# A new order and a new choice of engines for a two-layer attention and mixer kernel

## The chip, the cores and the metric

The kernel runs on one core of one Trainium2 chip. The metric is the device time of one execution in microseconds (us): 437.09 us for the kernel before, the median of three runs (436.16 to 437.51). One execution was also profiled; every time below that is not called a run's time comes from that one.

The engines are written as in the profile: PE multiplies matrices (PEld loads its weights), ACT, DVE and POOL work on elements, SP issues the DMA transfers. The engines run side by side. Each takes its own instructions strictly in order, and an instruction may wait on semaphores that other engines or transfers raise.

## What is computed

Two layers, each a sliding-window attention block and a token-mixing MLP, over one sequence of 2048 tokens with 512 features (cut to what matters):

```python
def _A_ref(x, wqkv, wo):                      # H = 32 heads of 16, window 256
    qkv = ((x @ wqkv).reshape(B, S, 3, H, Dh)).transpose(2, 0, 3, 1, 4)
    q, k, v = qkv[0], qkv[1], qkv[2]
    scores = jnp.einsum("bhqd,bhkd->bhqk", q, k) * (Dh ** -0.5)
    mask = (idx[:, None] - idx[None, :] >= 0) & (idx[:, None] - idx[None, :] < W)
    p = softmax(where(mask, scores, -1e9))
    return (einsum("bhqk,bhkd->bhqd", p, v)).transpose(0, 2, 1, 3).reshape(B, S, D) @ wo

def _B_ref(x, w1, b1, w2, b2):                # mixes along the tokens; F = 1792
    u = gelu(einsum("bsd,sf->bdf", layernorm(x), w1) + b1)
    return (einsum("bdf,fs->bds", u, w2) + b2).transpose(0, 2, 1)

x = A_x
for _ in range(2):
    x = x + _A_ref(layernorm(x), A_wqkv, A_wo)
    x = x + _B_ref(layernorm(x), B_w1, B_b1, B_w2, B_b2)
```

## The kernel before, in words

The program first records a graph of 2476 operations (`Graph.op`). An operation is one or a few instructions on one engine, with what it reads and writes; some operations have alternatives (`alts`) on other engines. The string `ORDER` then says in which sequence all operations are put down and, for each, which alternative is taken. `Graph.replay` follows it: it appends each operation to its engine's list and gives out the buffers (eight PSUM banks, pools of SBUF tiles) in that sequence. `Graph.emit` writes the lists out with the waits that the data and the reuse of buffers need. So `ORDER` alone decides the order on every engine, the engine of the operations of free choice, and which earlier user a buffer waits for. No cost is read at this point: the costs in the code were of use to the search that made the string, which is not part of the kernel.

The operations that the text speaks of, in the order in which a block of tokens meets them:

- x and the projection weights are loaded at the start (`load_x` L401, `load_w` L405; the weights of Q, K and V come in pieces: K first half, Q first half, V, K second half, Q second half, a half being 256 columns, that is two of four groups of eight heads).
- Layer norm: statistics L471 and L473 on DVE, the inverse root L484 on POOL, the normalised block L491 on DVE.
- The normalised block is transposed: for the first 512 tokens of layer 0 on PE (L549) with a copy out of PSUM on DVE (L556) or ACT (L558), later by a DMA (`tr`, L542).
- Projections on PE (L513). Q goes out of PSUM by DVE (L572) or ACT (L574). K goes straight into the buffer `kbd` (two instructions, DVE L583 or ACT L582), or into a staging tile `stg` (DVE L594, ACT L596) and from there into `kbd` by POOL or DVE (L609, two instructions) or by eight DMAs of SP (L604). V goes out by DVE (L631) or ACT (L633) and then by four DMAs into `vb` (`vz`, L636).
- Attention goes in 152 score operations on PE (L690). Each fills two pairs of PSUM banks; two exponentials on ACT (L705) empty them into a tile of `pt`. Masks (L726) multiply parts of `pt` on POOL or, with an AND, on DVE. When all parts of a group of heads are there, PE multiplies by V (`pv`, L747). DVE transposes the result (L767), takes a reciprocal (L771), POOL or DVE forms the product (L773), DVE transposes back (L778). PE applies `wo` (L513) and DVE adds to x (L789).
- The mixer: partial sums over the tokens that are ready (`u_part`, L513, out by DVE L853/L857 or ACT L855) are filled in between; the last part (L868) follows after attention, then an addition (L879, DVE), gelu (L883, ACT), and the second product (L513) with its addition to x (L909, DVE). The weights come in by SP (L803, L815). In layer 1 the results go out block by block (L955, L898).

PE never waits for PE. The score operations keep ACT busy, and everything else on PE is put between them, so that ACT has scores to work on and PE has something to do while ACT works.

Of the kernel before, what the change touches and what calls it, by code (L numbers as in the profile page):

```python
# [11 lines left out]
P = 128  # L12


ORDER = (
    'c-qBQJ&5a87Cw^iym#m24ro9DE$D$>P@zHr1r$&~4;*kn0Tl{p!G#}q!G!|~IH1A-2lN&PwBQ9TIN-tyE*x;-!V50EV3sLdcwrV?xbVUhQ@EI7Sf+5{!o?nq'
    '$20ciz5Hx8yJyB%_g-CH-SeIAd`ALMAW$=FmRTW@UM>_MC=^Pi;EO_mPE}Ps8;@00Q*G-bFh2xcf8YPD^Jy4{4r?wJVNeNZF(i;5j)u<AALc&kTb8BtuoYXD'
    'EV9&YSZ!4!>!g`bN{ewkFV?-!CZqniE{d#Ft%9xV!b#)(TCEaPYV5=_a)q2Md&JD;Y}-<ZEX(4%qNtz|nGh-nqM(nNFd2`>41lrbFj=oV>y08w5=@sO5l;Q9'
    'E5~t`4k7c4g`?**4MwApcs`k)PYEH@>2%p2_m%ug%J;zU^<}w}Bmj_HTwbUu%%gUDrPRKHF)ZpZ8V-j>IkgT#q9zGxwOWL+*Q6H5QAD5FVugcBIS8UCVtAx5'
    'oJ<&u19$iv7cna1#_*YKJ5^OyJ|z~OtkC_q)3F@aao}aY-|XcJja+V-4ePd#=6Nr5$8=54^GwtKgfnf&d1+c%n=zA#x^CzI129br?M|l+Elo!hRD}YZf_Qqu'  # L20
    'SP)3ERD?p|W-T+p<AlWmmz&J>+$%~ixu#_`=S`xiFBAY-2B_6)1cnJql2x_3URO7ptD9B5K6*wd)Vkd{-aVgQFQ<Q>cFUdVVsW`#OsA3K%;)o&*{hi55Q9-J'
    '&$FfBG&||^{?_aDDLp%bAP7veKNy<kcP63}C9PHz{n0aH$ElgsxDhjE)LBq-b-g0Gt{ca(`sEk$b^TQ&DrE65;-xkz7100?E&w~1%|a*V<m_xVrnDCQ9!bX-'
    'm1YXX*h}M)fU!Om&@okIOl(PvC5<{j12J|S3bq}Tigu~!`;_{gMNNZdeg7q;j;bwzsGwS!B?u~0Ziq%Y!^?{V8oI8Zce{fD0`^>Em^H0dLzbj46plFn<Ww=A'
    'FQK`4LOj>DNP1RH&t|jQXq06s1sG+39kbi*t^uyE!Cc~!i-kgzrhK_Xo{tGG>%nMzHqPfML1rY`Bx!fr#C02P^EJAFZ(cjutY58xXXjs)hPF-A3lBL3pX4lJ'
    'o4RQ@9~cBgQ$#}$1OcwgE@B2$AdHBjArra3DN3SFkg5WD1k-axgz>l%2E(u)1b&%$CBINMT;FsZMb~r1oPiq~IYiJfbj!AeLw#WAgbe9`w0dBuuGqvgRI6$j'
    'Lc4<2z`#YeO+!o3Fn0_>IzT9qQcL7U7do+6@7L?yx^*Vrn%pXe80Su@MFqwhm|>=H;=0V37#a(!ArlQI2rlNJAe`WqOfhG#%;{=H-5W~sx^x5=7q*a+gflh$'
    'eZw$Pt#TZr6a%Qw`y4VQmouyne9JOS0EC7qvVzDPj44PKNl{G8B<pp1eIlAyme0J)%S%H$)eL|an)+N(`aLv4B*F~_HO#v|s2W6@$RDsi$nbjkB_tw<aCUYk'
    '2%!wcfUen!F_|78BN06ngymAB$TM;-Nt5|()|t)vvzaWn&qvv;Tm`7MhvtWaKA@`N30<K-=(ly9A_Jd|R8$)In<f)_y+1(=bS0n$TwlMwx<cq7j=u@(C`omM'
    's+WpyhcVx0`At5b6!LM*{CvrmDw0$xmkNc#rysW*%d#2dEs#FcKqmsA;wpwx&^1K`SfV3>fB;P<6ID1nqf~>FlQsVIBw?qUO$1{_QR7&{n2;j^pNrDz@KvRP'
    'TuK<mIr4oZ1y_!9SyUwYJ76btI<*!T3yU5b?QZw{9Hy=d9K2`0HxPs}^t#>t;Lp8&uVtQFrU}$Q`lqt{ZNl~Yf`ICa&~-Y75XsujO{=A87$B%rB7GV}b(9zY'  # L30
    '!{`(WoNg6MMP0AzkT0PA69N(@pXYm16Wzfq^z*(fYqEw}a{7X?cLkw<Ig%y~Rv3X&ok}t$2N6%!f^;N~$NkaC$qf0x1Uyf>-6bt(Dr%$g90?}?KF5_9Bjq&r'
    '9VRfOm7H#+>+RW`V$C>FkB<j`i7}q|K(_<XYPW`Ah;7)b*Etl+sQ&d=xDeCKb@TZ=swXnG*RcqAC>3m#2FEZ|10}nJyGwXDa!fJMLOcUE@4D;t8rCTF_KdDp'
    '|1^yA<<&pVaphmfWICUu<!>~UB*XY_G#-s?$tqjlN}AScVXSKL*K!D9S_VJ=yjH4~LRu`AgEE#cl(BpvpVe)WwLK4sNQCSM`bXp=iwJ^1G+BAkm!89|;E<#0'
    '5m!-^W`k?os-6+90>f~bsiaDi{tQqkm1!RJ6VNdN6KJ;<Xrpm^*cw#FsDIU@*6DORRU@vZyI^4JQ7JM?MU+}7R=i5t^UGK(hjfISwCi<9P;1@T^KGmPwx6?$'
    '*`}Si72oo#we1*=ty>Z<K|oE*NRs|kQo3VFj-qBWDr2RP%}Py=YhYMbK*X6DDpU<N!bV@P(lwST5xh&(i+Q7GS|c{pKw4GeK!HfSMw)Ln+D&j%-rOMigkF)W'
    'tIbAOU&8!+J`XM&6!y_r8jXS!q*_hOK?T1v(t@EBna)rd<f<%4h$aS4NQ;jOl%l*~OW_w9_o&0&&v3hj+gnZ!duhI<*Czn)Jlx^9hb0`)bV%+FN`XV$Zku+n'
    '%>ZN|?LN&sO}kq=zHOhv-X((zp6<=U-J8*Pa_H5QU5DrIHq7vcHy#^*d!K)d4tMK5e>l${9Ua~EIN<K_y7Py7!t>njX^wjX)W6uc-L~877SOvn4xM=XCjR#3'
    'ffxM4i0An?kYc;%9Wwk|$-{APJ07>ksr#_L-FWzK8n-+D0aDygj{&!b@9tr^=Pk!^+<%y7KZ6b2k1gcj|6*(}X#Cwjf54*cklzn(I)3MF&FvFM_fPP5OiFd)'
    'PDWB$dFT6#-?q>0yM*KRNS1zT!}g1NyGbT<D<hdyr!twhb1?I;1+K~*&h7>o9{)0XkL(?vf4BgDKjPoOZ+@F@{L_OaPq}pBkzPEK;jMa+EjG7q-XVq8Cxq-~'
    'fqY-CA5M)9kj(yDwjO2Pn4mw1SmuWW<UnaM{7ypdNwS?t+e|9Z`@ub6^$)5i|0od;xd4x4`DbU#p|J1k!A{$`U5U8saSyKSuRIv-&+SBsdzd5tlMLqG#I842'  # L40
    'njg9Q>mP6%x*dvl<9p-|jZg3K-1a{$!)bv|s~^WdEIxed;iHG!)%)G|$*<zszX32A5e)'
)

def begin_order(n):
# [944 lines left out]
```

## Time and profile before

| what | value |
|---|---|
| median of three runs | 437.09 us (436.16 to 437.51) |
| the profiled execution, its time as a run | 436.27 us |
| its span in the profile | 434.5 us |
| granted PE clock | 1.00 in every stretch |
| busy: DVE, ACT, POOL | 322.6 us, 317.0 us, 187.2 us |
| DMA | 46.03 MB, mean 106 GB/s |

In the page of the profile the span is cut into 40 slices of 10.9 us; each digit is an engine's busy share in tenths. The span is shorter than the run's time by 1.8 us, which lies around the program and is not part of it. "Busy" of PE counts a matmul from its start to its modelled end, so that pauses shorter than a matmul's pipeline do not show as idle.

### The profile page before, as it was taken

To read this page: it belongs to the slowest core of one execution; us is meant where nothing else is said; L and a number is where in the kernel's file an instruction comes from. 1 tells how busy PE (TensorE), PEld (TensorE's weight loads), DVE (VectorE), ACT (ScalarE), POOL (GpSimd) and SP (SyncE) were. 2 spreads that over 40 slices of the span, in tenths; PEclk is the share of its full clock that TensorE was granted. 3 is DMA by queue.
4 is the path that set the end of the run, shared out by engine and by line. 5 is a ranking of instruction groups with operands and counts; after the bars stand their busy time and mean duration, and the time that the engine had idled before them with its cause. 6 is when DMAs were issued, how large, how long until landed. Compare 5 with 4: busy or idle time off the path is not lost.

```text
span 434.5 us, 14318 instructions
## 1 busy us (share of the span) xinstructions
PE 420.9 (97%) x6177; PEld 188.5 (43%) x6177; DVE 322.6 (74%) x629; ACT 317.0 (73%) x364; POOL 187.2 (43%) x277
## 2 busy tenths in 40 slices
PE   7979989999999999999999999999999999999997
PEld 6534333434444444444444444444434444445443
DVE  7998989779996678556777999989788758422205
ACT  5999999999997953606999999899999870520000
POOL 7788865864664620011465554365435221000000
PEclk9999999999999999999999999999999999999999
DMA  8565262302163257723542282240223262747713
GB/s 237 167 125 88 63 127 37 79 5 49 26 166 83 75 152 211 208 62 88 137 110 52 64 147 64 51 77 11 47 64 99 66 175 69 226 140 213 228 32 115
DMA packets 101850, 46.03 MB, mean 106 GB/s; under 512 B 32156, under 2 KB 101788, under 8 KB 101788
## 3 DMA queue, kind: packets, MB, share of 16 engines
q1 hardware_dynamic: 101788, 45.13, 41.7%
q8 instruction: 49, 0.80, 0.8%
q14 instruction: 13, 0.11, 0.1%
HBM read 33.56 MB, written 2.10 MB: 82 GB/s over the span
## 4 chain that ended last, share of the span: by engine, by line
PE 73%; ACT 18%; DVE 6%; DMA 1%; POOL 1%; issue 0%; SPq 0%
PE PS L513 50%; ACT pt L705 17%; PE PS L868 8%; PE PS L690 8%; PE PS L747 7%; DVE stats L471 1%; DMA vb<-vst 1%; DVE xh_sb L491 1%; DVE pt L726 1%; DVE rl L767 1%; DMA x_sb<-in_A_x_dram 1%; POOL pt L726 0%; DVE stg L594 0%; DVE vst L631 0%; SPq L636 0%
## 5 line engine op out<-in xcount | busy, mean ns | idle before, releaser
L705 ACT ACTIVATE pt<-PS 128x1024 bf16<-128x1024 f32 (+1 forms) x304 | 281.0, 1036 | 13.1 <-PE PS L690 11.9
L726 POOL TENSOR_TENSOR pt<-pt,ldm 128x256 int32<-128x256 int32 (+2 forms) x189 | 125.9, 686 | 101.7 <-ACT pt L705 101.1
L513 PE MATMUL PS<-xhT,wqkv 128*128 128x512 bf16 (+1 forms) x288 | 67.8, 357 | 2.7 <-ACT pt L705 1.9
L513 PE MATMUL PS<-xh_sb,w1b 128*128 128x512 bf16 x280 | 69.9, 381 | 0.1
L513 PE MATMUL PS<-uT,w2b 128*128 128x512 bf16 (+2 forms) x308 | 68.3, 360 | 0.0
L690 PE MATMUL PS<-qT,kbd 32*128 32x64 bf16 (+4 forms) x1552 | 60.2, 247 | 3.1 <-ACT pt L705 2.1
L484 POOL TENSOR_TENSOR rstd<-agg,mhalf 128x2 f32<-128x2 f32 (+1 forms) x33 | 23.8, 722 | 66.8 <-DVE agg L473 66.7
L909 DVE SCALAR_TENSOR_TENSOR x_sb<-PS,bcol,x_sb 128x512 bf16<-128x512 f32 x31 | 22.6, 746 | 38.0 <-PE PS L513 37.7
L690 PEld LDWEIGHTS PS<-qT,kbd 32*128 32x128 bf16 x1552 | 22.7, 92 | 61.7 <-ACT pt L705 45.6
L767 DVE STREAM_TRANSPOSE rl<-PS 128x1024 f32<-128x1024 f32 x32 | 39.9, 1248 | 12.3 <-PE PS L747 12.1
L747 PE MATMUL PS<-pt,vb 64*17 64x128 bf16 (+4 forms) x3104 | 43.6, 248 | 2.4 <-DMA vb<-vst 1.1
L471 DVE BATCH_NORM_STATS2 stats<-x_sb 128x6 f32<-128x512 bf16 x64 | 44.2, 693 | 1.5 <-DMA x_sb<-in_A_x_dram 0.8
L883 ACT ACTIVATE uT<-rl,bcol 128x512 bf16<-128x512 f32 x28 | 18.3, 712 | 33.8 <-DVE rl L879 33.8
L513 PEld LDWEIGHTS PS<-uT,w2b 128*128 128x128 bf16 x308 | 27.5, 98 | 31.1 <-issue 3.2
L747 PEld LDWEIGHTS PS<-pt,vb 64*17 64x17 bf16 x3104 | 31.8, 84 | 17.6 <-issue 7.9
L513 PE MATMUL PS<-uT,pt 128*128 128x512 bf16 x168 | 39.2, 379 | 0.0
L868 PE MATMUL PS<-xh_sb,w1b 128*128 128x512 bf16 x168 | 37.7, 379 | 0.0
L513 PEld LDWEIGHTS PS<-xhT,wqkv 128*128 128x128 bf16 x288 | 24.2, 97 | 30.1 <-issue 6.3
L513 PEld LDWEIGHTS PS<-xh_sb,w1b 128*128 128x128 bf16 x280 | 23.7, 98 | 30.8 <-issue 5.9
L513 PE MATMUL PS<-wqkv,xhT 128*128 128x512 bf16 x128 | 34.2, 381 | 0.2 <-DVE stg L594 0.2
L726 DVE TENSOR_TENSOR pt<-pt,ldn 128x256 int32<-128x256 int32 (+1 forms) x77 | 29.6, 404 | 5.3 <-ACT pt L705 5.0
L513 PE MATMUL PS<-wo_sb,oT 128*128 128x512 bf16 x128 | 32.4, 380 | 0.5 <-ACT pt L705 0.5
(62 smaller groups left out, 340.7 us busy)
## 6 DMA issues: line engine op xcount, KB each, us to landing
w1b<-in_B_w_dram SPq DMA_DIRECT2D x112, 128.0 KB, 2.8
w2b<-in_B_w_dram SPq DMA_DIRECT2D x70, 128.0 KB, 2.8
pt<-in_B_w_dram SPq DMA_DIRECT2D x42, 128.0 KB, 3.0
vb<-vst SPq DMA_DIRECT2D x64, 68.0 KB, 2.1
out_dram<-x_sb SPq DMA_DIRECT2D x15, 128.0 KB, 1.8
x_sb<-in_A_x_dram SPq DMA_DIRECT2D x3, 512.0 KB, 6.2
kbd<-stg SPq DMA_DIRECT2D x80, 16.0 KB, 1.9
wqkv<-in_A_wqkv_dram SPq DMA_DIRECT2D x4, 256.0 KB, 5.4
```

Of the source, the lines that this page charges most:

```text
L471: op("vector:stat", lambda e: e.bn_stats(st[:, 0:6], x_sb[:, t, :]), reads=[f"x{t}"], writes=[("st", i)], cost=dve_cost(512))
L484: op("gpsimd:rstd", lambda e: e.tensor_tensor(rstd[:, t0:t1, 0], agg[:, t0:t1, 1], mhalf[:, 0:1].to_broadcast([P, t1 - t0]), op=ALU.pow), ...
L491: op("vector:xh", lambda e: e.tensor_scalar(xh_sb[:, t, :], x_sb[:, t, :], agg[:, t, 0:1], rstd[:, t, :], op0=ALU.subtract, op1=ALU.mult), ...
L513: return e.matmul(o, lhsT=w, rhs=x, start=start, stop=stop, skip_group_check=True)
L690: last = e.matmul(bank(tt[r // 2], r % 2)[:, base + c0 * 64:base + (c0 + n) * 64], lhsT=kbd[32 * r:32 * r + 32, tk.slot, o, jj].rearrange( ...
L705: op("scalar:exp", lambda e, ts=ts, tp=tp, i=i, cols=cols: e.activation(probs(tp)[:, i, 0:cols, :], pair(ts)[:, :, 0:cols].rearrange("p r ...
L726: return e.tensor_tensor(v, v, m, op=by)
L747: last = e.matmul(bank(t, h)[32 * r:32 * r + 17, i + q0 * 64:i + (q0 + n) * 64], lhsT=vb[64 * h:64 * h + 64, tk.slot, jj, 4 * o + r, :], r ...
L767: op("vector:od", lambda e, t=tod, tr=tr: e.transpose(rl[:, tr.slot:tr.slot + 2].rearrange("p a b -> p (a b)"), pair(t)), reads=[(tod, i) ...
L868: last = e.matmul(bank(tu, tt), lhsT=v()[:, sc - b0, k0 + tt * P:k0 + (tt + 1) * P], rhs=xh_sb[:, sc, :], start=(sc == b0), stop=(sc == NT ...
L883: op("scalar:gelu", lambda e, ft=ft, tt=tt: e.activation(uT[:, ft, :], rl[:, tmps[tt].slot], ACTF.Gelu_apprx_tanh, bias=b1col[:, ft:ft + 1 ...
L909: op("vector:resy", lambda e: e.scalar_tensor_tensor(x_sb[:, t, :], bank(ft), b2col[:, t:t + 1], x_sb[:, t, :], op0=ALU.add, op1=ALU.add), ...
```

## The change

Only the string `ORDER` differs: the sequence of the 2476 operations and the alternative of each were found anew, in a search in which all larger transfers and all operations of free choice were assumed to take longer than measured.

```diff
 ORDER = (
-    'c-qBQJ&5a87Cw^iym#m24ro9DE$D$>P@zHr1r$&~4;*kn0Tl{p!G#}q!G!|~IH1A-2lN&PwBQ9TIN-tyE*x;-!V50EV3sLdcwrV?xbVUhQ@EI7Sf+5{!o?nq'
...
+    'c-p;IL5S<t6}`{%{O8Tj8_)*@6wn8KP(T4Kl%jxAR8T-4Tu?v@1)SoA0}g26fC3IU;DRX*IK=^f&_Wa!TyVfGF3iG|S$N@v3r=xi0$$8w3NCozfD5yjg$uLj'
...
 )
```

Decoded, the choices of engine that change (operations, not instructions):

| operation | before | after |
|---|---|---|
| K out of PSUM into `stg` | ACT 3, DVE 24 | ACT 4, DVE 23 |
| K out of PSUM into `kbd` | ACT 4, DVE 5 | ACT 2, DVE 7 |
| Q out of PSUM | ACT 7, DVE 29 | ACT 10, DVE 26 |
| V out of PSUM | ACT 5, DVE 27 | ACT 7, DVE 25 |
| partial sums of the mixer out of PSUM | ACT 3, DVE 39 | ACT 2, DVE 40 |
| `stg` into `kbd` | POOL 12, DVE 5, SP 10 | POOL 12, DVE 6, SP 9 |
| masks | POOL 189, DVE 77 | POOL 183, DVE 83 |
| products L773 | POOL 18, DVE 14 | POOL 23, DVE 9 |
| ones in `vst` (L458) | POOL | DVE |

PE has the same 6177 matmuls in both, and its list has the same number of changes between kinds of work: 142 from a score operation to projections or mixer, 121 the other way, 31 from `pv` to a score operation, 27 into `pv`, and so on, all equal. The sequence differs nearly everywhere in detail. The start, decoded (the operations of one engine from left to right, `sc` a score operation, K0 to K3 and Q0 to Q3 the projections of the four groups of heads, V a half of a V projection, T a transposition on PE; a token half follows in brackets where it is the second 256 tokens):

```
SP  before  x1 x0 x2-3 K01 Q01 x4-7 Q23 K23 V  b1 b2 x8-11 w1 w1 x12-15 vz tr tr tr tr wo w1 vz
SP  after   x1 x0 Q01 x2-3 K01 Q23 x4-7 K23 V  x8-11 b2 w1 w1 w2 w1 w1 b1 x12-15 w1 vz tr tr tr tr w1 w1 vz wo
PE  before  T1 T0 K0 Q0 Q1 K1 sc T3 T2 Q3 sc Q2 K2 sc K3 V b V sc V V Q3(2) sc Q2(2) sc Q0(2) K0(2) K2(2) K1(2) V sc
PE  after   T1 T0 K0 Q0 Q1 K1 sc Q3 T3 K2 T2 Q2 K3 sc Q2(2) V V sc V V sc K0(2) V V K3(2) sc K1(2) b Q0(2) sc
ACT before  L558 L558 L582 L574 L574 L596 L705x3 L574 L705x7 L574 L705x2 L582 L705 L633 L705x13
ACT after   L558 L582 L574 L574 L596 L705x2 L558 L574 L705 L596 L574 L705x5 L633 L705x2 L582 L705x17
```

More of the change, by code (lines that the diff above doesn't have):

```diff
@@ L15 @@
 ORDER = (
-    'c-qBQJ&5a87Cw^iym#m24ro9DE$D$>P@zHr1r$&~4;*kn0Tl{p!G#}q!G!|~IH1A-2lN&PwBQ9TIN-tyE*x;-!V50EV3sLdcwrV?xbVUhQ@EI7Sf+5{!o?nq'
-    '$20ciz5Hx8yJyB%_g-CH-SeIAd`ALMAW$=FmRTW@UM>_MC=^Pi;EO_mPE}Ps8;@00Q*G-bFh2xcf8YPD^Jy4{4r?wJVNeNZF(i;5j)u<AALc&kTb8BtuoYXD'
-    'EV9&YSZ!4!>!g`bN{ewkFV?-!CZqniE{d#Ft%9xV!b#)(TCEaPYV5=_a)q2Md&JD;Y}-<ZEX(4%qNtz|nGh-nqM(nNFd2`>41lrbFj=oV>y08w5=@sO5l;Q9'
-    'E5~t`4k7c4g`?**4MwApcs`k)PYEH@>2%p2_m%ug%J;zU^<}w}Bmj_HTwbUu%%gUDrPRKHF)ZpZ8V-j>IkgT#q9zGxwOWL+*Q6H5QAD5FVugcBIS8UCVtAx5'
@@ L20 @@
[L20 to L39, printed above, removed]
@@ L40 @@
-    'fqY-CA5M)9kj(yDwjO2Pn4mw1SmuWW<UnaM{7ypdNwS?t+e|9Z`@ub6^$)5i|0od;xd4x4`DbU#p|J1k!A{$`U5U8saSyKSuRIv-&+SBsdzd5tlMLqG#I842'
-    'njg9Q>mP6%x*dvl<9p-|jZg3K-1a{$!)bv|s~^WdEIxed;iHG!)%)G|$*<zszX32A5e)'
+    'c-p;IL5S<t6}`{%{O8Tj8_)*@6wn8KP(T4Kl%jxAR8T-4Tu?v@1)SoA0}g26fC3IU;DRX*IK=^f&_Wa!TyVfGF3iG|S$N@v3r=xi0$$8w3NCozfD5yjg$uLj'
+    '^~9dB=l`VnP3WDmB|Y7D-@Esmd!A!i0QPAepkf+^5#~!J8s+n09&(fd3*H-fo+R~{^A2r;^>+S)I_F$aX;g|>%X-_IOeXxo(}EzE6Ak0Uu>8O^O;?DY8gCj&'
+    '>&<fG)4CzjdP5W$9pK#JqA;D-YBk}JB#lno^3#FeeNCg(39?y*HL8(UtOkKBvruBM+Ad>`ZRrLT1WmsZR0Ra4s0tUw`OFZ8LqQlafesSd>^7U6_pTIKYAvNm'
@@ new lines @@
+    'TFj*x|A+7M<#Jgnc^(Th)9KW4I&IqTpPlt5=*-8Hadwi0pso%EgLZF8mwsBow8hC}dAY3DDwV2Mu4&-HXbhnY4LHf?&=S&Ww?t8Fz1#9?)dna4QB<i&Qn8qh'
+    'LpcmdwN?!alu}NI;b0JkAqD51Tn=oTdhdcC`2H`SIxROzM()rYv|Y!v?M4H~Eh}r8zUTS=ugoB8J~bV8`2b(qj_Wv%i3J2f(*PJqf9v%nqX%8R)zU@X&;@~W'
+    'RZ~F(I4%~8AW2d#cd0DZz~xSkOhsl28TWWTZ-Hqsl0Iw5bx8)`7>%)VIsSJUpxG=#Y5C9PY(8Ji=iPQ8tkp`nY`Y4JI9>vbE@tz;jz&q6i>K%37hj*b2)B89'
+    'Iv5UyqoGqMO!2PYKP{X}lGE?tn0aj$P6q|E*L-H0*`!uWlEgHFATX0wQZso_EPq<!Tr8E<C<s&$xuL37AqW;9lq(m(dqHqD2|o;jLRf(CPiCXh_=^_+fa3zR'
@@ new lines @@
+    'U9=`+wpsm+WpR@;NnzuO2*N-Zh>rwC(X@6OlE<9KaSV{OIAzpvTo>%fMh@o)ZiG^%8-;?aQ_ZGGTWULsdVS4Q%4A9fSyt)A<9R&qw@=zkl2qDg*Sp<%LsgXH'
+    'S0za(M(K6Wa2|%mFw3)7H0x(P@I2QC7`wV|T)M-d3$nC^hn$?805>|sxQ6A5f5UanFjgyQCxGB09Kw{35$7aMk~r>l{~Uh_6#16RBcGDQ67x>{S*?a_K#~=U'
+    'H2NfPe8<VY9|Rf77&y8uX*wW1tC1v1J*g~7qSzKi9K!Gs7JyPk@?B}zs8cYcTo#8Z%|kt3pmyG&5$Hxv)EzU>1db_%hJmRn%4(%xC#srOwNz7+WD_Js&eCAc'
+    '6sg~mdI{%k5JV)CRf5PbMo|>U#X3_3j=Ob$S~*!ZWEmSwluXO)^?Iy(TJLmv^?E&NL933`u&iOOKZs-wOkitkJp01sc;(#l^h_q>WhTB+I+i&LX`w(>m9fj!'
@@ new lines @@
+    '3UkW1?xR!Mx9xX+;k0QQBVpIr)hhMhLQ(S!md@KWZOL*mA44vi>ARXIsj6w(U>S-5x~|EBAQRLcw3_^y@yNKk0zt*zdV@{jjJyW$2t+I@9JQORRtu8)?~W0w'
+    'QmG9P!u241Dl3<la^sr@mQ;tDfEEP0d<-B+jzD3-ebgk*$MgAI6c)>cdc=q{lBVaVPCfbW^0+k^IL=UhTtdl`3K*pWUjhLnKs&Z=NK7!G5j1;3qt_J#-4X<q'
+    '(Jt+hTJ;Kd8<*$v^5>*hDpgCUNVrs)^OKVT3If8RHK7Cwi6Eqz9FoQr6^f#R@?sf5U}<YWfeK^QR#mXDfQs@4ybhByO;?dq61<99(d~AR1W{O`9{h_#tu}%R'
+    'qbN3uMXfcL<qAwes6@g?$iQJTz(V*D<2a$r5@@;&_jC6{d^8NAbE`L*9E}TKnb@79w}!*u=SW1HaRR@GB%pCZX#+R+41y*eP7j)m7+WHK_J#ZzT^kl<wOVN!'
@@ new lines @@
+    'RTs@BrF96yN@b`N3fS3L{yaYCbE+!p7}E7TB?E>5Cg_Z*uQRoeD%kxaZoDdC|3{RDn#Q@pa0|F~+ZH%A@SwRygB6~VqBIx?3{GaVnZ{HV+qkXiNdjy8EzS@T'
+    'u6+I&n2q;Gx~?B-$d#X&MCf!n=NIQV!g;f)%#{9VzfaTjOWNsn0KpAAAtn~KDwVK)c3v(gN$5CXq0o3=$rnx2E9CQ*13}iX4AcizT}l%6AAj;hl;y|adVMS}'
+    'WJ%Tug4NaX^78Vg-9&`&Z29$ad3FYLj1W06`U=H+gj+SFLBIWnzTVSuvmH^a*Q6#iy1iff9whMb$Db5GDjt=EX{o?UP|RfTCjt2RylXg4&dFvG4cjuY7iEyv'
+    '$DH{3lk+FyV^NG{XtO5L{t?O<l`bMuD#0YW!b8I0H>H9#z!kAQVQj>ay8xmfj28Hd0HBY0S&C=?KBgQNqXePM7n@Po&96bF46;EHicUVC4;Z$buZIrsQ*~^u'
@@ new lines @@
+    'Pe^;sSVyD?y;e2?Gt^AWRefL6G+E7<MMG6pnpI__1y^NRVV9Ja@w#BNN}bi>dckV!(w;4sAZt#}R;}6WY9<cA!gjb^&iHIGo0o)1eN6jsb>&~PTDH(a6`S(#'
+    '0_eFHd8gj!<RpM@J@FScYd)`Ks&SlIsbf5Gob}IyT7*YwGEE>Xg;5v=Ss|x;1uqsdn(LzatW6WtwQ%6Uj5-7qdze%Bkw!Mx2ZzGl7$NJ=;e$QT^v3ZHth>9t'
+    'ZP1&)y(I|QMn1$3-7ax(c>5CX$sroR!P*hO4mZ;e5BGO`a6s>8{QzJy_8>)5o557-z7K37f4||pbn1SQwh6qTemALX9lp(FJ#=$R?n(+j-pF38+mM@u$o=sx'
+    '9Q39Vsm=FpqT8ob>cylW_=4<>?7O`%tJ`gSN6M+~Uj83OzW4FPQ}#i-mklAiiIE=`@_7VbV%F`-KV3DR4|UA{$B=6%Q+LKw8&;)m{`X<ul5TCUq+Z$gxT^`d'
@@ L42 @@
+    '<J>Oe$sQ9Q(ueSn(1+wkYSx-UVNZ8%eh6#?<5oI$x}V-^!NJxG1!>=B=V`|^wbMU$u~R#jEx%L1QuoSm(`z?_>2ICUH;tdey)uyJb^T8CD3EQH$nJYeHd4I4'
+    '(lp$c&0VQJI5^m;&H8DlNH0>#gXeT}KXdwASEu$-zsY(}eqhU$4fN#Y`gBij$+lO?a{@)+<>PKVzm@hE>)q{=JH*|{KG_q&?Z7UH@05hx2@1Kl+)sIIke8B='
+    '+p3WtP&4v!A-^j?>c2)OJ4&!E8X;Sdcj~xxCAZ)ZlG;?4?ACtcOUREqF<#3412nG=iv'
 )
```

## The prediction

> **What bounds the kernel now.** I read the first page for the busy shares and the chain of waits, then the busy times by stretch, then the chain in order of time, then PE, ACT and DVE over the first 50 us.
>
> ```profile
> PE 420.9 (97%) x6177; PEld 188.5 (43%) x6177; DVE 322.6 (74%) x629; ACT 317.0 (73%) x364; POOL 187.2 (43%) x277
> PE   7979989999999999999999999999999999999997
> ACT  5999999999997953606999999899999870520000
> PE 73%; ACT 18%; DVE 6%; DMA 1%; POOL 1%; issue 0%; SPq 0%
> ...
> 20.00:60.00 40.00, 35.81 (x814) 15.44 (x806) 37.11 (x76) 39.06 (x44) 31.93 (x46) 1.00 0.50 92
> 60.00:100.00 40.00, 37.78 (x786) 15.90 (x782) 32.62 (x58) 39.60 (x44) 26.52 (x39) 1.00 0.27 57
> 100.00:140.00 40.00, 39.68 (x781) 17.26 (x781) 34.76 (x67) 36.30 (x40) 23.23 (x33) 1.00 0.34 86
> ```
>
> In the last three lines the columns are stretch, length, then busy time of PE, PEld, DVE, ACT, POOL. PE sets the time almost everywhere, but not from 20 to 100 us: there ACT works 78.66 of 80 us and PE has 6.4 us of holes. DVE is close behind from 20 to 60 us (37.11 of 40). From 100 us to the tail PE has at most 0.65 us of holes in any 40. So PE's matmuls are a fixed sum, and an order can only change the holes, 13.6 us in all (434.5 - 420.9) and most before 100 us, and the shorter waits that a matmul's modelled end hides.
>
> ```profile
> 28.60 4.01 DMA vb<-vst
> 32.65 1.52 PE PS L747 x114
> 34.57 1.03 ACT pt L705
> 43.98 36.82 ACT pt L705 x40
> ```
>
> These are pieces of the chain that ended last (start, length, what). Around 30 us it runs through the V transfer into `vb`; from 44 us, 40 exponentials stand back to back, 0.92 us each. What delays ACT before 44 us delays the end, as long as ACT then has no rest to make it good.
>
> **What does not change.** Both lists of PE have the same 6177 matmuls and the same changes between kinds of work, so PE's work is priced at no difference. The moves of engine nearly cancel. ACT loses two K pairs of 512 columns (4 x 0.65 = 2.6 us, row L582) and one mixer copy (0.6), and gains a 256-column K copy (0.37), three Q copies (3 x 0.62) and two of V (2 x 0.59): +0.2 us. POOL loses 6 masks (0.74 each) and the 0.65 us of ones, gains 5 products (1.06): +0.2. DVE gains 6 masks (0.44), two K pairs (1.5 each), one K write (0.68), the mixer copy (0.69) and the ones (0.17 as its other fill, L394, to 0.65 as on POOL), and loses 5 products (0.75), three Q and two V copies (0.68 each) and a K copy (0.41): about -0.4. Most of the moves lie in layer 1, where PE covers them. What counts is where the waits fall.
>
> **Step 1, the first weights.** SP now asks for Q's first half before x2-3, and for Q's second half before x4-7; K's second half stays eighth. Nine transfers were served in order before; the second K half took this long from issue at 4.35 us:
>
> ```profile
> wqkv<-in_A_wqkv_dram SPq DMA_DIRECT2D x1, 256.0 KB, 6.8
> 9.71 0.62 PE L549 MATMUL PS<-ident,xh_sb 128*128 128x128 bf16 x8 [0.37 <-DVE xh_sb L491]
> 10.37 0.61 PE L513 MATMUL PS<-xhT,wqkv 128*128 128x256 bf16 x4
> 10.97 0.29 PE L690 MATMUL PS<-qT,kbd 32*128 32x128 bf16 x8
> 11.19 1.05 PE L513 MATMUL PS<-xhT,wqkv 128*128 128x256 bf16 x8
> ```
>
> It landed at 11.15 us, with the same bytes ahead of it in both orders. Before, PE used it at 11.53, behind the second score operation (10.97). After, PE meets K2 in front of T2, Q2, K3 and that score operation. Up to the first score operation (8.95) nothing moves: K's first half becomes the fifth transfer, and the fifth landed at 7.06, just ahead of its use at 7.11. Then Q3 9.28, T3 9.71, and K2 waits to 11.2: a hole of 1.2 us where before there were 0.6 (T3's wait for L491 and Q3's for its weights). From there by the rows: K2 0.43, T2 0.22, Q2 0.43, K3 0.43 and 0.1 for the change of kind put the second score operation at 12.8, 1.85 us later. Bounds: the half lands one 256 KB place sooner (10.3) or at the place of V behind it (12.5); I take 11.15, its place in the queue.
>
> One operation here is not shown in the trace: the copy of the second transposed block (T0) out of PSUM by DVE, from 6.41 us, while POOL fills `kbd` until 7.79. DVE's other copy of this kind took 0.40 us. At the dear end it stands until the fill ends, as the mask arithmetic did here:
>
> ```profile
> 6.41 1.43 DVE L433 TENSOR_SCALAR ldm<-tri,half 128x64 int32<-128x64 bf16 x1
> 5.99 1.80 POOL L461 MEMSET kbd<- 128x2048 f32 x1
> ```
>
> That end moves K0 from 7.11 to 8.3, +1.2 us. I take the cheap end: one of the two copies of that form ran beside a POOL operation (L609, 9.52 to 10.46) and both took 0.40. [...]
>
> **Step 2, ACT.** It idles from 11.25 to 12.1 (T2's end, where before it had an exponential at 11.31), then 0.1 and 0.16 at the next two score operations: 1.1 us. It also does two things more among the exponentials: a transposed block's copy (0.59; before at 6.38, when ACT was idle anyway) and a K copy (0.37). Less 0.1 of its own idling before, ACT is 1.9 us late when the first score operation of the second chunk is emptied (24.5 against 22.5).
>
> **Step 3, the holes of before.** Until 44 us ACT before had three holes between exponentials: 0.27 at 24.4 us, 0.89 at 33.7 and 0.34 at 43.6 (distance of two starts less 0.9), together 1.5. The second is the wait shown by this row:
>
> ```profile
> 32.65 1.52 PE L747 MATMUL PS<-pt,vb 64*17 64x64 bf16 x128 [1.06 <-DMA vb<-vst]
> ```
>
> After, DVE copies that V out ahead of L767 instead of behind it, at 23.2 to 23.9. SP issues the first V transfer, four transposes (1.3 each) and two mixer loads (0.5 each) first, then these four DMAs at 26.1; 2.6 to issue and 3.4 to land give 32.1, and PE wants them at 33.7. That hole goes. New ones come where DVE is late: PE gets its four K and Q projections ahead of the same score operation (0.3), and the transposes L767 and copies of DVE hold it (0.05 and 0.2): 0.55. ACT is then 1.9 - 1.5 + 0.55 = 0.95 late at 44 us.
>
> **Step 4, from 44 to 100 us.** ACT stays full, and from 49 us on PE's order is nearly the same in both: the 0.95 goes through. SP now writes two more K blocks (8 DMAs, 5.6 us each) ahead of the four transposes of the third quarter; from the issue rows the latest of these lands near 78 us, the first projection that wants it stands near 87: covered, and 5 us late would still cost nothing.
>
> **Step 5, behind 100 us.** I followed each chain that leaves PE (a score operation, its exponentials, mask, `pv`; or `pv`, L767, product, L778, `wo`; or a load) and comes back, and set its rows against PE's work beside it. The worst beat PE by 0.42, 0.09, 0.07, 0.21, 0.27, 0.90 and 0.08 us in seven stretches; before by 0.50, 0.09, 0.07, 0.06, 0.21, 0.90, 0.05. That is +0.15. Chains through loads miss by over 0.9 us in both. The tail ends with 128 columns in place of 256: the last addition takes 0.35 in place of 0.48, -0.13.
>
> **Sum.** 0.95 + 0.15 - 0.13 = +1.0 us: a span of 435.5 against 434.5. The profiled run (436.27) lies at the low end of the runs; the difference is put on their median: 437.1 + 1.0 = 438.1. A difference under 0.3% (1.3 us: 435.8 to 438.4) is about what cannot be told from none.
>
> **Rivals.**
> - *The start is made good* (437.1). ACT's lateness is taken up between 60 and 100 us, where ACT has 0.4 us to spare and PE 2.2 us of holes. For: PE's fillers may bridge it. Against: 36.82 us of exponentials in one piece.
> - *Faster* (435.5). The landing at 10.3 saves 0.85, no new holes open (0.55), and the 1.2 us by which PE waits between 100 us and the tail (L747, L513 and L690 for L705, L513 for L594) go: 438.1 - 0.85 - 0.55 - 1.2. For: V and the third quarter's transfers get more room. Against: the chains of step 5 have no more room than before.
> - *Clearly slower* (440.3): DVE takes over from ACT up to 45 us. After, a Q copy and L767 release two score operations around 35 us with less than 0.1 us to spare; x4-7 lands 0.9 later than before (10.3 against 9.42) and DVE's statistics with it, and collisions with POOL cost up to 0.5 each (a mask on DVE: 0.415 median, 0.949 longest). From 0.1 us on each delay goes to ACT whole: 0.9 + 2 x 0.5 + 0.3 = 2.2 more. For: 37.11 of 40 us busy. Against: half of DVE's work there is statistics for later blocks.
>
> **How the numbers follow.** Forecast 0.50 (half of it under 438.4), made good 0.17, faster 0.15, DVE 0.18. Faster 0.15, same 0.25 + 0.17 = 0.42, slower 0.25 + 0.18 = 0.43. The forecast's own range is 437.3 to 439.4; with the rivals and the two bounds of step 1 (-0.85; +1.2 and +1.4) it is 435.4 to 440.6.
>
> **What would show it.** After: a wait of PE of about 1 us at L513 near 10 us and the second score operation at 12.8 (step 1); ACT idle near 11.5 and 1.9 us late at 24 (2); no wait of L747 for `vb` near 33 (3); 40 exponentials in one piece, 0.95 later (4). It is wrong if K2 does not wait, if ACT has idle time between 44 and 95 us, or if PE has holes behind 100 us that a load or DVE ended.

## The result, and the profile after

The changed kernel took 437.9 us (median of 21 runs, 436.64 to 440.61), the kernel before, run on the same chips, 436.85 (21 runs, 435.56 to 438.35). The ratio is 1.0028, 95% interval 1.0014 to 1.0041: 1.05 us longer by the medians (the ratio is not that of the two medians). A later comparison on another chip gave 437.84 against 436.33, ratio 1.0028 (1.0011 to 1.0045). In about a third of the executions of either kernel (32 of 92 before, 11 of 33 after) the mean granted clock is 0.992 to 0.996 in place of 0.999 or 1.000; in the profile after, one of them, PE ran at half speed for 3.41 us at the start (the last section). Where no such stretch is on record the medians of that comparison are 437.48 and 436.21, so the order's own difference is about 1.3 us. Three single runs of experiments (527.5, 592.9 and 1422.6 us, one each of the second, fourth and eleventh) stand far outside all others and are left out of the medians and ratios below.

The first page of the profile after (busy time, PE and ACT in 40 slices, shares of the chain of waits) and its stretches answer to the lines shown of before:

```profile
PE 413.5 (95%) x6110; PEld 188.1 (43%) x6177; DVE 320.0 (73%) x632; ACT 316.6 (73%) x365; POOL 188.4 (43%) x275
PE   7979988999999999999999999999999999999997
ACT  3999999999998852704989999999999970430000
PE 74%; ACT 21%; issue 2%; DMA 1%; SPq 0%; DVE 0%
...
20.00:60.00 40.00, 34.37 (x813) 15.97 (x820) 36.63 (x77) 39.71 (x46) 32.74 (x48) 1.00 0.45 93
60.00:100.00 40.00, 36.57 (x726) 15.09 (x732) 33.35 (x61) 39.72 (x44) 24.01 (x35) 1.00 0.24 50
100.00:140.00 40.00, 38.36 (x772) 16.65 (x762) 34.67 (x66) 38.31 (x43) 24.05 (x34) 1.00 0.32 79
```

PE's busy time can't be set against that of before: 67 of its 6177 matmuls have no record here (x6110), and each gap counts as "issue". What can be read is ACT. From 20 to 100 us it now works 79.43 of 80 us, 78.66 before. It has no rest there, and yet it is late.

This execution (438.24 us, span 436.4) had the half-speed stretch, as PE's timeline (start, length, line, shapes, count, idle before and what ended it) and its stretches (the 0.50 is the granted clock) show:

```profile
7.41 3.54 PE L513 MATMUL PS<-xhT,wqkv 128*128 128x256 bf16 x16 [1.19 <-DMA wqkv<-in_A_wqkv_dram]
...
8.00:9.00 1.00, 1.00 (x6) 0.73 (x5) 0.89 (x5) 0.54 (x2) 0.47 (x1) 0.50 1.05 309
```

Sixteen matmuls took 3.54 us; before they took 1.9. A second profile of the changed kernel had it too (0.50 from 8.6 to at least 12 us). The order at full speed is seen best in the first experiment, whose first 68 us are the changed kernel's. There PE's timeline at the start and the chain of waits (start, length, what) read so (line numbers of the experiments are up to two off; L688 is L690, L703 is L705):

```profile
7.06 1.92 PE L511 MATMUL PS<-xhT,wqkv 128*128 128x256 bf16 x16 [0.63 <-DVE xhT L554]
8.92 0.40 PE L688 MATMUL PS<-qT,kbd 32*128 32x256 bf16 x12
9.69 0.39 PE L547 MATMUL PS<-ident,xh_sb 128*128 128x128 bf16 x4
11.68 0.60 PE L511 MATMUL PS<-xhT,wqkv 128*128 128x256 bf16 x4 [1.59 <-DMA wqkv<-in_A_wqkv_dram]
13.30 0.29 PE L688 MATMUL PS<-qT,kbd 32*128 32x128 bf16 x8
```

```profile
4.35 7.20 DMA wqkv<-in_A_wqkv_dram
...
21.14 9.18 ACT pt L703 x10
...
34.01 1.95 ACT pt L703 x2
...
45.49 27.61 ACT pt L703 x30
```

PE waits 1.59 us for K's second half, the second score operation starts at 13.30 (10.97 before), and the chain runs through that transfer. There is no wait for `vb` in it any more. The exponential that starts at 43.98 before starts at 45.49, 1.5 us later.

### The profile page after: what moved, and what is told of

It is laid out like the page before. It is cut to its first block, busy times and chain, and to the rows that moved or that the text cites. A ratio compares the mean times of both kernels' runs of the same rounds, so it can differ in the third digit from the quotient of the medians.

```text
span 436.4 us, 14255 instructions
## 1 busy us (share of the span) xinstructions
PE 413.5 (95%) x6110; PEld 188.1 (43%) x6177; DVE 320.0 (73%) x632; ACT 316.6 (73%) x365; POOL 188.4 (43%) x275
## 4 chain that ended last, share of the span: by engine, by line
PE 74%; ACT 21%; issue 2%; DMA 1%; SPq 0%; DVE 0%
PE PS L513 52%; ACT pt L705 21%; PE PS L868 8%; PE PS L690 8%; PE PS L747 7%; DMA wqkv<-in_A_wqkv_dram 1%; SPq L401 0%; ACT qT L574 0%; ACT kbd L582 0%; ACT stg L596 0%; ACT vst L633 0%; ACT xhT L558 0%; SPq L405 0%; DVE x_sb L895 0%
## 5 line engine op out<-in xcount | busy, mean ns | idle before, releaser
L705 ACT ACTIVATE pt<-PS 128x1024 bf16<-128x1024 f32 (+1 forms) x304 | 281.3, 1059 | 9.5 <-PE PS L690 8.3
L726 POOL TENSOR_TENSOR pt<-pt,ldm 128x256 int32<-128x256 int32 (+2 forms) x183 | 122.6, 688 | 96.1 <-ACT pt L705 95.6
L513 PE MATMUL PS<-xhT,wqkv 128*128 128x512 bf16 (+1 forms) x270 | 66.5, 363 | 6.1 <-ACT pt L705 2.6
L513 PE MATMUL PS<-xh_sb,w1b 128*128 128x512 bf16 x265 | 66.6, 380 | 2.5 <-issue 1.8
L690 PE MATMUL PS<-qT,kbd 32*128 32x64 bf16 (+4 forms) x1552 | 60.2, 247 | 4.1 <-ACT pt L705 3.0
L690 PEld LDWEIGHTS PS<-qT,kbd 32*128 32x128 bf16 x1552 | 22.5, 92 | 63.2 <-ACT pt L705 44.1
L767 DVE STREAM_TRANSPOSE rl<-PS 128x1024 f32<-128x1024 f32 x32 | 39.9, 1247 | 12.7 <-PE PS L747 12.5
L747 PE MATMUL PS<-pt,vb 64*17 64x128 bf16 (+4 forms) x3104 | 43.8, 248 | 1.6 <-ACT pt L705 1.0
L471 DVE BATCH_NORM_STATS2 stats<-x_sb 128x6 f32<-128x512 bf16 x64 | 43.4, 684 | 2.1 <-DMA x_sb<-in_A_x_dram 1.3
L513 PE MATMUL PS<-uT,pt 128*128 128x512 bf16 x163 | 41.2, 379 | 0.3
L726 DVE TENSOR_TENSOR pt<-pt,ldn 128x256 int32<-128x256 int32 (+1 forms) x83 | 31.5, 397 | 11.7 <-ACT pt L705 11.4
L747 PEld LDWEIGHTS PS<-pt,vb 64*17 64x17 bf16 x3104 | 31.8, 84 | 16.8 <-ACT pt L705 7.6
L868 PE MATMUL PS<-xh_sb,w1b 128*128 128x512 bf16 x164 | 38.3, 379 | 0.3 <-issue 0.2
L513 PEld LDWEIGHTS PS<-xhT,wqkv 128*128 128x128 bf16 x288 | 24.5, 100 | 31.8 <-issue 6.7
L513 PE MATMUL PS<-wqkv,xhT 128*128 128x512 bf16 x120 | 32.4, 380 | 1.1 <-issue 1.0
L773 POOL TENSOR_TENSOR ul<-rl,rc 128x512 bf16<-128x512 f32 x23 | 24.7, 1076 | 20.0 <-DVE rc L771 19.8
```

Source lines behind the costliest of these rows:

```text
L471: op("vector:stat", lambda e: e.bn_stats(st[:, 0:6], x_sb[:, t, :]), reads=[f"x{t}"], writes=[("st", i)], cost=dve_cost(512))
L513: return e.matmul(o, lhsT=w, rhs=x, start=start, stop=stop, skip_group_check=True)
L690: last = e.matmul(bank(tt[r // 2], r % 2)[:, base + c0 * 64:base + (c0 + n) * 64], lhsT=kbd[32 * r:32 * r + 32, tk.slot, o, jj].rearrange( ...
L705: op("scalar:exp", lambda e, ts=ts, tp=tp, i=i, cols=cols: e.activation(probs(tp)[:, i, 0:cols, :], pair(ts)[:, :, 0:cols].rearrange("p r ...
L726: return e.tensor_tensor(v, v, m, op=by)
L747: last = e.matmul(bank(t, h)[32 * r:32 * r + 17, i + q0 * 64:i + (q0 + n) * 64], lhsT=vb[64 * h:64 * h + 64, tk.slot, jj, 4 * o + r, :], r ...
```

## The experiments

All were timed against the kernel before on the same chip in five rounds, with 12 runs each (six in the sixth and the ninth to eleventh). "Late" is the start of an exponential against that of the same number before, each from one profile: the first of the second chunk (22.54 us before) and the one at 43.98 us.

**Which part of the order.** The first takes sequence and engines of the changed kernel up to the score operation near 68 us and those of before behind it, the second the other way round.

```diff
 e1  all engines, up to the score operation near 68 us
-  order of before
+  order of after
 e2  all engines, behind it
-  order of before
+  order of after
```

> The changed order up to the score operation that stands near 68 us, the order of before from there on. If the loss arises before 45 us (K2 in front of the second score operation, the first transfers, two more copies on ACT), it is all here: ratio to before 1.0025 (1.0015 to 1.004), ACT about 1 to 1.7 us late at its 40th exponential. If it comes from the moves of engine in layer 1, the ratio is 1.000 (0.999 to 1.001).

> The order of before up to the same score operation, the changed order from there on. If the loss arises before 45 us: ratio 1.000 (0.999 to 1.001), exponentials up to the 60th as before. If layer 1 costs it: 1.0025. If the changed order is better behind 68 us (the faster rival): below 0.999.

The start alone: 437.59 against 436.45, ratio 1.0017 (0.9997 to 1.0036), span 436.0. The rest alone: 437.29, 1.0029 (1.0009 to 1.005), span 435.6. So the rest is not free, as it should have been if all of the loss arose before 45 us, and the times of the two overlap. The profiles tell more. With the new start ACT is 2.0 us late at 22.54, 1.5 at 43.98 and still 1.47 at the last exponential, with the old rest. With the new rest alone PE falls behind by 0.5 us where the two orders meet (50 to 60 us), by 0.35 near 212 us at a V transfer, and by 0.35 between 215 us and the end (compared at the same amount of PE's work). The last of these, or more, appears in each profile of the second to sixth and the eighth, and not in the first experiment. The 0.5 where the orders meet belongs to the mixture alone, so the parts do not add up to the whole.

**The loads, and K2's place.** In the third the first nine transfers stand in the order of before; in the fourth, K2 and K3 stand behind the second score operation.

```diff
 e3  SP
-x1 x0 Q01 x2-3 K01 Q23 x4-7 K23 V
+x1 x0 x2-3 K01 Q01 x4-7 Q23 K23 V
 e4  PE
-sc Q3 T3 K2 T2 Q2 K3 sc Q2(2) V V sc
+sc Q3 T3 T2 Q2 sc K2 K3 Q2(2) V V sc
```

> The changed order with its first nine transfers in the order of before. K's first half lands near 5.6 us instead of 7.3, so the first projection starts at 7.1 instead of 7.4 and PE's clock does not fall to half there. If the transfers are the whole loss: ratio 1.000. If K2's place on PE and the copies on ACT are the larger part, as the prediction has it: 1.0015 (1.0005 to 1.0025), with the second score operation still at 12 to 13 us. If they matter nothing: 1.0028.

> The changed order with K2 and K3 of the first 256 tokens behind the second score operation on PE. If K2's wait for its weights delays the chain: the second score operation comes 1 us earlier against the first (2.5 us behind it instead of 3.8 at full clock), ratio 1.000 to 1.0012. If ACT's two extra copies or DVE set the start, nothing is won: 1.0025 to 1.003.

With the loads back: 437.74, ratio 1.0027 (1.0009 to 1.0046). Its profile shows ACT 1.15 late at 22.54 us instead of 2.0 and a span of 435.2, but that execution was the fastest of its twelve; by the medians nothing is gained, so a gain isn't shown. With K2 behind: 437.76, 1.0036 (1.0017 to 1.0056). Here the second score operation starts at 11.65 instead of 13.30, and ACT is still 1.8 late at 22.54. Taking 1.65 us from the wait gave ACT 0.24. One reason stands in PE's timeline: at 18.4 us ACT was still 0.85 ahead of the first experiment, and then PE waited for a K copy on DVE.

```profile
19.69 0.61 PE L511 MATMUL PS<-xhT,wqkv 128*128 128x256 bf16 x4 [0.72 <-DVE kbd L581]
```

In the first experiment this wait is 0.17. The edit also put K2's copy on DVE behind six statistics operations, so PE's list was not the only one to change. The wait for K2 is real, but it isn't by itself what makes ACT late: DVE sets the next limit.

**The changed kernel again, and the two copies.** The sixth puts the copy of T2 and that of K3 on DVE again; the eighth does the same with the loads back.

```diff
 e6, e8  engine
-evt T2  ACT    evk K3  ACT
+evt T2  DVE    evk K3  DVE
```

> The changed kernel once more, for a profile whose granted clock is 1.00 all through and for a comparison on the same chip. In the first profile of it, one window of 3.41 us (7.37 to 10.78) ran at a granted clock of 0.50. Theory (the lateness of ACT at the start is the order's own, not the window's): with the full clock the first exponential starts at about 9.4 as before, the one that starts at 24.62 before starts about 1.75 later, and the span is about 435.9; ratio 1.003. Rival (the half-clock window is what made the changed kernel longer): the exponential at 24.62 is less than 0.5 late and the span is within 0.4 of 434.5.

> The changed kernel with two copies (the transposed block T2, 0.59, and a K projection, 0.37) on DVE again instead of ACT. Theory (ACT sets the time up to 100 us, and each thing it does more among the exponentials goes to the end whole): ACT is 0.8 to 0.96 less late at 24 us and the time falls by that, to about 436.7, ratio about 1.0005. Rival (the second score operation is what is late, and the copies lie in ACT's wait for it): no change against the changed kernel, 437.6. Rival (DVE is the tighter engine there): slower than the changed kernel.

> The changed kernel with the first nine transfers in the order of before and the two copies on DVE again. Theory (both parts of the start add): ACT is 0.88 late at 24.6 us with the loads alone, so about 0.0 to 0.1 late with the copies back too, and ahead of before by about 0.4 at 44 us, since the hole of V is closed and 0.9 of new holes stand against 1.5 of before. The span is then 434.5 - 0.4 + 0.4 (the part of layer 1) = 434.5, the time that of before, 436.5. Rival (the copies lie in waits): 437.6, as with the loads alone.

The changed kernel again: 437.84, span 436.6, ACT 2.5 late at 22.54, with a half-speed stretch once more, so that the profile at full speed that this run was for is missing. The copies back: 439.66, ratio 1.006 (1.0037 to 1.0084), 1.8 us longer than the changed kernel. The eighth: 439.11, 1.0054. DVE's timeline of the sixth, and then PE's, say why:

```profile
12.69 0.42 DVE L592 CAST stg<-PS 128x256 bf16<-128x256 f32 x1
13.02 1.28 DVE L469 BATCH_NORM_STATS2 stats<-x_sb 128x6 f32<-128x512 bf16 x2
14.22 0.25 DVE L471 BATCH_NORM_AGGREGATE agg<-stats 128x2 f32<-128x9 f32 x2
14.38 0.65 DVE L469 BATCH_NORM_STATS2 stats<-x_sb 128x6 f32<-128x512 bf16 x1
15.04 0.38 DVE L554 COPY xhT<-PS 128x512 bf16<-128x512 bf16 x1
15.34 0.41 DVE L592 CAST stg<-PS 128x256 bf16<-128x256 f32 x1
```

```profile
12.28 0.39 PE L547 MATMUL PS<-ident,xh_sb 128*128 128x128 bf16 x4
15.48 0.61 PE L511 MATMUL PS<-xhT,wqkv 128*128 128x256 bf16 x4 [1.72 <-DVE xhT L554]
```

T2 is on its way out of PE by 12.7, but its copy starts at 15.04, behind six statistics operations (L469, L471) that stand ahead of it in the list; PE waits 1.72 us for it. A change of engine without a new place in that engine's queue is another experiment than the one meant. The changed order could afford the statistics there because ACT took the two copies.

**V early, alone.** The seventh is the kernel before with the second block's V out of PSUM ahead of a reciprocal and a statistics operation, and its transfers ahead of two loads. The statistics operation (686) went behind L767.

```diff
 DVE
-K stat(686) rec V stat V agg L767
+K V rec stat V agg L767 stat(686)
 SP
-tr tr tr tr wo w1 vz
+tr tr tr tr vz wo w1
```

> The kernel before with one thing of the change alone: V of the second block goes out on DVE ahead of a reciprocal and a statistics operation, and its four transfers stand ahead of two weight loads on SP. Theory (the wait of L747 for vb is a hole of ACT, and closing it counts to the end): the transfer is issued 0.8 earlier, the hole of 0.89 between the exponentials near 33.7 falls to about 0.1, ACT is 0.75 earlier from 35 to 100 us and the span ends 0.6 to 0.8 earlier, 436.45 - 0.7 = 435.75, ratio 0.998. Rival (another wait takes its place by 44 us): the exponential of 43.98 is less than 0.2 earlier, the time the same.

436.21 against 436.33, ratio 0.9996 (0.998 to 1.0012): no difference. Its timeline of PE at the hole of before, and later:

```profile
32.19 1.53 PE L745 MATMUL PS<-pt,vb 64*17 64x64 bf16 x128 [0.63 <-DVE qT L570]
...
213.43 1.05 PE L745 MATMUL PS<-pt,vb 64*17 64x64 bf16 x72 [0.22 <-DMA vb<-vst]
```

L747 no longer waits for `vb` but for a Q copy on DVE, which ended at 32.14 instead of 31.59, as the statistics operation that I moved now stood ahead of it. Half of the hole remains (0.47 of 0.89). ACT is 0.46 early from 36 to 206 us (the theory had 0.75), and then about 0.3 of this is lost in layer 1 to a V transfer that landed 3.8 us after its issue (3.4 before). This loss belongs to the one execution: in the twelfth, which has the same order, the transfer took 3.5 and nothing was lost.

**The half-speed stretch.** The ninth and tenth put 13 more matmuls into PE's waits at the start, in the kernel before and in the changed one, to see whether the stretch goes when PE works there. With that the author expected 109 ns for every projection, and for the ninth a median of 435.9 to 436.1. The eleventh has the loads back too, with the two copies on DVE behind their projections, ahead of the statistics.

```diff
 def f_tr(e):
     for c in range(4):
         last = e.transpose(...)
+    for _ in range((7, 6)[t] if t < 2 else 0):
+        e.matmul(PS[:, warm.slot, 0:P], lhsT=uT[:, 0, 0:P], rhs=uT[:, 0, 0:P], start=True, stop=True)
     return last
```

> The kernel before with 13 more matmuls of the warm-up's kind (128 columns, result unused) in PE's two waits at the start: 6 behind the transposition of T1, 7 behind T0. [...] Rival (the fill itself delays T0 or K0): all runs 0.2 to 0.7 longer.

> The changed kernel with the same 13 matmuls. Theory: the half-speed window goes here too, the runs draw together, and what is left is the order's own difference: first exponential at 9.4 to 9.8, the exponential of 24.62 about 1.7 late, span 435.8 to 436.1, median 437.2 to 437.5, about 1.3 above the filled kernel before. Rival (the window was the larger part of the difference): median within 0.5 of the filled kernel before.

> The changed kernel with the first nine transfers in the order of before, the two copies on DVE straight behind their projections and ahead of six statistics operations (which stood ahead of them in the run with both), and the fill. Theory (the two copies were late there because of what stood ahead of them on DVE, and of ACT's two extra copies only K's 0.37 delays it, as T2's 0.59 lies in its wait for the second score operation): the exponential of 24.62 is 0.4 to 0.6 late, span 434.8 to 435.1, median about 436.6. Rival (both copies count whole): 0.0 late, span 434.4 to 434.6, median 436.1. Rival (the statistics, now later, delay layer norm and transfers): over 1.0 late at 24.6 or 44 us.

The projections ran at 109 ns in all three profiles, and yet the kernels were longer: 438.97, 439.71 and 439.19 against 436.79 (ratios 1.0053, 1.0069 and 1.0065), and two of six runs of the tenth had the stretch on record. The tenth is 0.74 above the ninth, between the 1.3 of the theory and the 0.5 of the rival. For the ninth neither 435.9 to 436.1 nor 0.2 to 0.7 longer fits. Its waits of PE, by what ended them (total, times, longest):

```profile
PE PS L511 <- issue: 1.5, 2, 1.0
...
PE PS L690 <- issue: 0.9, 2, 0.4
```

PE stood still for 2.3 us (the rows are rounded) in four stops that nothing on record ended ("issue"), 1.0 of it at 90 us; before there is no such wait. In the tenth (two stops) and the eleventh (three) it is 1.1 us each; in the tenth this is only part of the 1.9 us by which it is longer than the changed kernel was in its own second comparison. The stops of the ninth come behind 1217, 3265, 4801 and 6081 of PE's recorded instructions (weight loads, matmuls and semaphore instructions), and those of the other two at the same numbers, the first two in the tenth, all but the second in the eleventh. Between the four lie 2048, 1536 and 1280 instructions: 8, 6 and 5 times 256. The fill moved PE's instructions by 26 places. A stop took 0.2 to 1.0 us. That PE waited for instructions there is the author's guess; what it waited for is not shown. In the eleventh the exponential of 24.62 was 1.5 late, over the 0.4 to 0.6 expected and as late as the last rival has it, with PE waiting 0.9 for Q's second half at 10.4 us: whether either of the two copies counts stays open.

**The fill without moving instructions.** The twelfth is V early with the fill, and with as many instructions as before: eleven warm-up matmuls are twice as wide, eleven are left out.

```diff
-for _ in range(36):
-    last = e.matmul(PS[:, warm.slot, 0:P], lhsT=uT[:, 0, 0:P], rhs=uT[:, 0, 0:P], ...)
+for k in range(25):
+    n = 2 * P if k < 11 else P
+    last = e.matmul(PS[:, warm.slot, 0:n], lhsT=uT[:, 0, 0:P], rhs=uT[:, 0, 0:n], ...)
 def f_tr(e):
+    for _ in range((7, 4)[t] if t < 2 else 0):
+        e.matmul(PS[:, warm.slot, 0:P], lhsT=uT[:, 0, 0:P], rhs=uT[:, 0, 0:P], start=True, stop=True)
```

> The kernel before with V of the second block early (as alone before) and with PE's two waits at the start filled again (4 and 7 matmuls), but with no instruction more on PE: eleven of the 36 warm-up matmuls are 256 columns wide and eleven narrow ones are left out there, so that from the first projection on each instruction has the place in PE's list that it had before. Theory (the fill keeps PE at full speed, and what made the filled kernels 2 us longer were PE's waits for nothing but instructions, at the same four places of its list in all three): no such wait in the profile, projections at 109 ns, hardly a run above 437, median 435.6 to 436.0, ratio 0.998 to 0.9995. Rival (the fill delays by itself, or more matmuls bring the waits): 438 or more. Rival (the fill does nothing): about a third of the runs above 437, the median as with V early alone, ratio 0.9996.

436.36 (435.86 to 437.52, 12 runs; 435.6 to 436.0 expected) against 437.11, ratio 0.9974 (0.9952 to 0.9996): shorter than the kernel before, by an interval that ends just under 1, and in one comparison alone. One of its runs is above 437, eleven of the 17 of before beside it are; none of its runs has the stretch on record, eight of those 17 do. PE's timeline at the start:

```profile
5.48 0.63 PE L551 MATMUL PS<-uT 128*128 128x128 bf16 x4
6.33 0.56 PE L551 MATMUL PS<-uT 128*128 128x128 bf16 x7
7.26 1.91 PE L512 MATMUL PS<-xhT,wqkv 128*128 128x256 bf16 x16 [0.38 <-ACT xhT L559]
```

The fill stands in the two waits, the projections take 1.91 us, and none of the four places shows a stop. (66 matmul records are missing in this profile, and it has "issue" waits of up to 0.2 us at the gaps.) The gain is that the longer executions are gone: against those of before without the stretch, 436.44 here and 436.2 over all comparisons, it is next to nothing, although ACT is still 0.37 early at the last exponential of the profile. The run has V early and the fill together, and no run has this fill alone.

## Why the prediction was right, step by step

The sum, +1.0 us and 438.1, came out as +1.05 and 437.9 (by the medians; +1.5 in the later comparison), or +1.3 where no half-speed stretch is on record. The steps were less exact than their sum, and that they met it is in part luck.

- **Step 1** was right in kind, and its bounds held. K's second half landed at 11.54 in the first experiment, so that PE waited 1.59 us in place of 1.2 and the second score operation came at 13.30, not 12.8. This is one execution: in the six profiles with these loads the half landed between 10.61 and 11.77, and the 11.15 taken lies in the middle. DVE's copy of T0 was cheap, as taken: it took 0.41 us beside POOL's fill, as the profile after shows.

```profile
6.41 0.41 DVE L556 COPY xhT<-PS 128x512 bf16<-128x512 bf16 x1
5.86 1.80 POOL L461 MEMSET kbd<- 128x2048 f32 x1
```

"Nothing moves up to the first score operation" held in the first experiment (K0 at 7.06), but not in the two profiles of the changed kernel: there K's first half landed at 7.28 and 7.65, and K0 began at 7.41 and 7.78. A landing 0.05 us ahead of its use was too close to call nothing.
- **Step 2** was right in its number: 24.5 predicted, 24.56 measured for the first exponential of the second chunk (the first experiment). Its reasons are not shown. The fourth experiment took 1.65 us from PE's wait and ACT gained 0.24; the two copies, priced at 0.96, brought nothing in any of the three runs that took them off ACT. Lateness at 24 us isn't the sum of a wait and two copies; several limits lie close together, DVE's among them.
- **Step 3** was right about V: no wait of L747 for `vb` is left near 33 us, though V early alone closed only half of that hole. The new holes of ACT were mis-sized: 0.55 predicted, 0.93 measured (0.34 at 34, 0.14 at 36, 0.45 at 45.5 us). The hole before the 43.98 exponential was counted as going, and it is there again. So ACT was 1.5 late at 44 us, not 0.95.
- **Step 4** was right: 45.49 against 43.98 at the start of the run of exponentials, 1.51, and 1.44 at 96 us. The chain of the profile after has the piece "45.76 36.78 ACT pt L705 x40", that of before "43.98 36.82 ACT pt L705 x40".
- **Step 5** was low: behind 215 us each profile with the new rest lost 0.35 or more, where +0.15 was predicted for all seven stretches. So PE does not cover all of the moves in layer 1. Only about 0.1 of this shows as a hole (at 293 us in the second profile of the changed kernel, ended by DVE's L767); the rest lies in waits that the modelled ends hide, and what they wait for stays open. The tail gained 0.16, near the 0.13 predicted (from the start of the last matmul to the end 2.95 before, 2.79 after).

So the terms that were too small, 0.4 of holes and 0.2 of layer 1, would give +1.6. The profile of the first experiment is a long execution of its kind, though: 437.68 against a median of 437.07 where no stretch is on record, which is 0.96 above the 436.11 of before beside it. 0.96 for the start, 0.35 for layer 1 and about -0.1 for the tail make +1.2, near the 1.3 measured. That the late landing of K's second half made this execution long is likely, but not shown.

Of the rivals, "the start is made good" falls: ACT's lateness of 44 us is there at 96 and at the end. "Faster" falls with it; the gain of V is real and the start costs more. "DVE takes over" was not the outcome, but it named a real danger: PE waits for DVE up to 15.5 us in the sixth experiment, once two copies went there, and up to 19.7 us in the fourth.

## What to carry to other kernels

A hole closed on the engine that sets the time is worth its length only as long as every later transfer and queue moves up with it: V early gave half of its hole, as the next wait stood close behind, and in one of two profiles most of that was lost 180 us later. Before an operation goes to another engine, read what will stand ahead of it in that engine's list; its own 0.4 us may start 2.4 us late. And a sum of small terms that comes out right can hide steps that do not: check them one by one in a profile of part of the change.

## What was not expected of the hardware

**PE's speed at the start differs from execution to execution.** From one start to the next a matmul of 256 columns takes 109 ns (before, from 7.11 us) or 213 ns (after, from 7.41 us), one of 128 columns 56 or 107 (both in the warm-up after). In the profile after, the warm-up matmuls ran at 107 ns up to 3.9 us, then at 56, and the projections at 213 from 7.37 to 10.78 us: 3.41 us, at a granted clock of 0.50. In the second profile of the changed kernel the change up came at 5.18 and the one down at 8.6, 3.42 us later. In both, PE waits for T0 (0.47 and 0.44 us) and for K0 (1.19 and 1.42) in the 3.4 us ahead of the slow stretch; in the profile before the two waits are 0.47 and 0.77, and no slow stretch follows. What sets the speed is not shown: the projections ran at 109 ns in all four profiles with a fill, but two of six runs of the tenth have the stretch on record. The stretch is on record in 32 of 92 executions of the kernel before, whose median is then 437.7 in place of 436.2: 1.5 us.

**The granted clock doesn't show all of it.** In the eighth experiment all matmuls up to 10.4 us ran at half speed, 213 ns for each projection, under a granted clock of 1.00 in every stretch:

```profile
7.05 3.44 PE L511 MATMUL PS<-xhT,wqkv 128*128 128x256 bf16 x16 [0.52 <-DVE xhT L554]
```

In the twelfth PE came up at 6.3 us, by its matmuls, and no stretch shows it either. So the counts of executions with the stretch on record are lower bounds. The durations of equal matmuls say it; the clock column doesn't.

**PE can stand still with nothing on record to wait for.** Adding 26 instructions to its list at the start brought stops of 2.3, 1.1 and 1.1 us in three kernels, at the same places of the list, multiples of 256 apart; a like fill without a shift (11 matmuls in place of 13) brought none. What PE waited for, and why just at these places, isn't shown.
